# A recurrence with a per-channel decay, then a Fourier mix: one running sum less in batches 2 and 3, its exponentials moved one partition down by a DMA

## The chip, the core and the metric

The kernel runs on one core of one Trainium2 chip. The core has five engines with their own instruction streams: TensorE (PE in the profile; its weight loads are PEld), VectorE (DVE), ScalarE (ACT), GpSimd (POOL) and SyncE (SP), which here only issues DMAs. Sixteen DMA engines move data between HBM and the on-chip memory SBUF, which has 128 partitions; TensorE writes to PSUM, of eight banks. The metric is the device time in microseconds; a run's time is that of the whole execution, and the profile's span reaches from its first instruction to its last.

## What is computed

Two steps, one behind the other, on 4 batches, 8 heads, 768 steps and 48 channels a head (8 x 48 = 384).

```python
for t in range(S):
    cur = einsum('bhd,bhe->bhde', u * k[t], v[t])
    y[t] = einsum('bhd,bhde->bhe', r[t], state + cur)
    state = w[t][..., None] * state + einsum('bhd,bhe->bhde', k[t], v[t])
# y laid out as x: batch x 768 x 384
mixed = real(fft(fft(x, axis=1), axis=2))
un_ = x + mixed
un  = (un_ - mean) / sqrt(var + 1e-6)              # over the 384
out = un_ + maximum(un @ w_ch1, 0) @ w_ch2         # 384 -> 1536 -> 384
```

## The kernel before

**Tiling.** A batch is cut into six chunks of 128 steps, which lie on the 128 partitions. Chunks are counted through, n = 6b + c, so that batches 2 and 3 are n = 12 to 23. Batch 0 is worked in pairs of chunks by a function of its own (`attention2`); all others go through `attention`.

**A chunk in `attention`.** ScalarE takes the logarithm of w into a bf16 tile (L931). TensorE multiplies it by two triangles of ones, which gives two running sums over the steps: with MSK the sum over the steps before t (tile `tce`, L933), with NLE minus the sum up to and with t (tile `tci`, L937). A further small matmul puts the chunk's total into eight more columns of `tci` (L946). ScalarE takes the exponential of `tce` where it lies in PSUM (L939) and that of `tci` into the SBUF tile E2 (L952). r is multiplied by the first exponential (L971, VectorE, since that operand is in PSUM) and k by the second (L974, on GpSimd or VectorE). Both products are transposed, in batches 0 to 2 by TensorE (L987, L993), in batch 3 by a transposing DMA (L979). Then come their product A (L1003), its masked copy `ah` (L1008), the state (L1029, decayed at L1037), y (L1050 and L1053) and the sum into the row buffer X (L1059). Beside that, r times k times u is summed into `dc` and multiplied with v.

**Folding and mixing.** `fold` adds and subtracts mirrored columns of X. `mix` does the Fourier step with matmuls against cosine and sine tables (L1117, then L1140), adds X into a tile UF (L1142), takes its mean and variance (L1146, L1148), subtracts the mean (L1152), transposes (by TensorE in batches 0 and 1, by DMA at L1169 in 2 and 3), multiplies by W1 (L1187), applies the relu when it moves the result to SBUF (L1194 on ScalarE or L1192 on VectorE), multiplies by W2 (L1205), adds UF (L1209) and writes a row block out (L1213). There are two X and two UF buffers, by the parity of the batch.

**Inputs.** Each chunk's w, k, r, v is one load of 192 KB (L587) into one of seven slots; W1 and W2 are loaded by GpSimd's DMA queue (L745), W1 asked for once a load of batch 0 has landed and its turn on GpSimd has come.

**The order.** `op()` records every operation with the engines that it may run on, a cost, what it reads and what it writes. The table ORDER lists, for each engine, the numbers of the operations in the order in which that engine issues them; the number is the place in which the program recorded it. Nothing is ordered at run time: an engine stops at an operation until the semaphores of what it depends on have come, and everything behind it in its list waits too. The costs are used only to place PSUM tiles in banks and to sort the waits. SP's list has 120 DMAs.

Of the kernel before, what the change touches and what calls it, by code (L numbers as in the profile page):

```python
# [7 lines left out]
ALU = mybir.AluOpType  # L8
# [15 lines left out]

PAIRED = (0, 2, 4)
# [33 lines left out]
    "act": (  # L59
# [13 lines left out]
    "dve": (  # L73
# [15 lines left out]
    "pool": (  # L89
# [11 lines left out]
}  # L101


class _Tile:


    __slots__ = ("bank", "ops", "pool", "n_done", "end")

# [1173 lines left out]
```

## Time and profile before

| | |
|---|---|
| median of 3 runs | 186.04 us (184.61 to 190.06) |
| profiled execution, its time | 187.16 us |
| profiled execution, its span | 185.4 us |
| DMA engines, share of the span: queue of SP | 64.8% |
| DMA engines, share of the span: queue of GpSimd | 6.7% |
| mean granted TensorE clock | 0.989 |

The span is what the views divide; the time has the start and the end of the execution around it. A busy TensorE is not a TensorE at its peak, since the ends of matmuls are modelled and overlap, so the distance between the starts of neighbouring matmuls in an unbroken run is the better measure of what one costs. A share of the DMA engines is the time that packets took, summed over the sixteen and divided by sixteen times the stretch.

### The profile page before, as it was taken

How to read it: one execution, taken by the hardware profiler on the slowest of the kernel's cores; microseconds unless marked ns; L12 is line 12 of the kernel's file. 1: busy time of each engine (PE TensorE's matmuls, PEld its weight loads, DVE VectorE, ACT ScalarE, POOL GpSimd, SP SyncE). 2: the span in 40 equal slices, each digit the busy share in tenths (PEclk: the TensorE clock that was granted, in tenths of full speed). 3: DMA queues.
4: the chain of work that ended last, by engine and by line, in shares of the span. 5: the costliest groups of instructions: out<-in, count | busy, mean ns of one | idle time of the engine just before them, and what ended most of it. 6: DMA issues, size and time to landing. Idle time of an engine off the chain costs nothing.

```text
span 185.4 us, 4736 instructions
## 1 busy us (share of the span) xinstructions
PE 176.7 (95%) x1824; PEld 126.0 (68%) x1824; DVE 151.6 (82%) x360; ACT 128.7 (69%) x303; POOL 106.6 (58%) x128
## 2 busy tenths in 40 slices
PE   5999999997999999999999999999999999999993
PEld 2355676754788768767785777758788666887771
DVE  7979999999499999999999999999897297180043
ACT  5989999996799577899588789726745513627120
POOL 2359999799958826999694659868645000000000
PEclk9999999998799999999999999999999999999999
DMA  6999998999999899899498399692811005412033
GB/s 158 325 301 257 218 194 176 193 194 186 209 211 196 162 196 216 195 224 212 89 213 174 70 234 164 116 183 56 205 46 42 4 0 139 117 42 88 0 127 127
DMA packets 102600, 29.01 MB, mean 157 GB/s; under 512 B 98865, under 2 KB 102066, under 8 KB 102450
## 3 DMA queue, kind: packets, MB, share of 16 engines
q1 hardware_dynamic: 102034, 26.36, 64.8%
q0 software_dynamic: 544, 2.36, 6.7%
q8 instruction: 14, 0.23, 0.5%
q14 instruction: 8, 0.07, 0.1%
HBM read 23.59 MB, written 4.72 MB: 153 GB/s over the span
## 4 chain that ended last, share of the span: by engine, by line
PE 74%; DVE 9%; ACT 7%; DMA 6%; issue 2%; POOL 1%; POOLq 0%; DVEq 0%; ACTq 0%
PE bank L1205 24%; PE bank L1187 24%; DMA w<-in_moe_w_ch_dram 6%; PE bank L1140 5%; PE bank L1117 3%; DVE ah L856 2%; PE bank L1003 2%; PE bank L1226 2%; PE bank L1053 2%; PE bank L1248 2%; ACT rkt L550 1%; PE bank L1050 1%; ACT lb L541 1%; DVE xf L527 1%; PE bank L933 1%
## 5 line engine op out<-in xcount | busy, mean ns | idle before, releaser
L1187 PE MATMUL bank<-unt,w 128*128 128x384 bf16 x288 | 57.5, 335 | 1.0 <-DMA w<-in_moe_w_ch_dram 0.8
L1194 ACT ACTIVATE ht<-bank 128x384 bf16<-128x384 f32 x88 | 39.9, 496 | 24.4 <-PE bank L1187 24.0
L1205 PE MATMUL bank<-w,ht 128*128 128x384 bf16 (+2 forms) x300 | 53.0, 320 | 0.0
L1187 PEld LDWEIGHTS bank<-unt,w 128*128 128x128 bf16 x288 | 38.5, 145 | 8.3 <-DMA w<-in_moe_w_ch_dram 1.0
L1205 PEld LDWEIGHTS bank<-w,ht 128*128 128x128 bf16 x300 | 28.0, 98 | 15.6
L1209 DVE SCALAR_TENSOR_TENSOR osb<-bank,rstd,uf 128x384 f32<-128x384 f32 (+2 forms) x25 | 14.4, 594 | 17.8 <-PE bank L1205 13.3
L1008 DVE TENSOR_TENSOR ah<-bank,msk 128x512 bf16<-128x512 f32 x36 | 23.2, 678 | 0.9 <-PE bank L1003 0.7
L527 POOL TENSOR_TENSOR rkh<-in_k,e 128x384 bf16<-128x384 f32 x20 | 19.9, 997 | 5.6 <-ACT e L952 5.3
L527 POOL TENSOR_TENSOR rk<-rk,ub 128x384 f32<-128x384 f32 x18 | 18.6, 1038 | 5.5 <-DVE rk L527 2.4
L527 POOL TENSOR_TENSOR vtd<-in_v,dc 128x384 f32<-128x384 f32 (+1 forms) x22 | 18.1, 827 | 3.7 <-DVE dc L960 3.7
L527 POOL TENSOR_TENSOR rk<-in_r,in_k 128x384 f32<-128x384 f32 x18 | 18.2, 1020 | 0.0
L541 ACT ACTIVATE un<-uf,agg 128x384 bf16<-128x384 f32 x20 | 12.1, 615 | 7.1 <-DVE agg L1148 7.1
L550 ACT ACTIVATE rkt<-bank 128x512 bf16<-128x512 bf16 x24 | 15.1, 633 | 1.6 <-PE bank L987 1.6
L527 POOL TENSOR_TENSOR sd<-x 128x385 f32<-128x385 f32 x9 | 9.4, 1046 | 11.2 <-DVE sd L527 5.4
L1142 DVE TENSOR_TENSOR uf<-bank,x 128x384 f32<-128x384 f32 x24 | 12.9, 549 | 2.4 <-PE bank L1140 2.2
L527 POOL TENSOR_TENSOR xf<-sd 128x382 bf16<-128x382 f32 (+1 forms) x9 | 10.4, 1164 | 4.5 <-DVE sd L527 4.3
L1146 DVE BATCH_NORM_STATS2 bst<-uf 128x6 f32<-128x384 f32 x24 | 12.7, 546 | 0.1
L939 ACT ACTIVATE bank<-bank 128x384 f32<-128x384 f32 x18 | 8.8, 493 | 5.7 <-PE bank L933 5.7
L1059 DVE TENSOR_TENSOR x<-bank,vtd 128x384 f32<-128x384 f32 x18 | 9.7, 547 | 3.3 <-PE bank L1053 3.3
L541 ACT ACTIVATE lb<-in_w 128x384 bf16<-128x384 f32 (+1 forms) x21 | 12.1, 576 | 0.3 <-PE bank L798 0.2
L541 ACT ACTIVATE vb<-in_v 128x384 bf16<-128x384 f32 x22 | 11.4, 532 | 0.0
L952 ACT ACTIVATE e<-bank 128x392 f32<-128x392 f32 (+1 forms) x18 | 8.9, 497 | 2.5 <-DVE bank L1037 1.1
(167 smaller groups left out, 356.4 us busy)
## 6 DMA issues: line engine op xcount, KB each, us to landing
out_dram<-osb SPq DMA_DIRECT2D x23, 192.0 KB, 2.3
in_w<-in_w_dram SPq DMA_DIRECT2D x18, 192.0 KB, 4.3
in_k<-in_k_dram SPq DMA_DIRECT2D x18, 192.0 KB, 4.0
in_r<-in_r_dram SPq DMA_DIRECT2D x18, 192.0 KB, 3.9
in_v<-in_v_dram SPq DMA_DIRECT2D x18, 192.0 KB, 3.8
w<-in_moe_w_ch_dram POOLq DMA_DIRECT2D x2, 1152.0 KB, 10.6
in_w<-in_w_dram SPq DMA_DIRECT2D x3, 384.0 KB, 4.6
in_k<-in_k_dram SPq DMA_DIRECT2D x3, 384.0 KB, 4.6
```

Source lines behind the costliest of these rows:

```text
L527: return lambda e: e.tensor_tensor(out=o, in0=a, in1=b, op=f)
L541: return lambda e: e.activation(o, a, f, **kw)
L550: {"act": lambda e: e.activation(o(), i(), ACTF.Copy), "dve": lambda e: e.tensor_copy(out=o(), in_=i())}, **kw)
L1008: masked[n] = op("dve", v_1(512), lambda e, x=x: e.tensor_tensor(out=ah[:, x:H:2, :], in0=ps(ta[x])[:, :].rearrange("p (h t) -> p h t", t= ...
L1059: op("dve", v_1(DM), lambda e: e.tensor_tensor(out=xb[:, c, 0:DM], in0=ps(ty)[:, 0:DM], in1=vtd[:, :, :].rearrange("t h d -> t (h d)"), op ...
L1140: return e.matmul(ps(t)[:, 0:DM], (hcs if kb < NP else HCR)[:, j, a:a + 128], DTM[:, j, :], start=(j == 0), stop=(j == 2))
L1142: op("dve", v_1(DM), lambda e, kb=kb, t=t: e.tensor_tensor(out=uf[:, kb, :], in0=ps(t)[:, 0:DM], in1=xb[:, kb, 0:DM], op=ALU.add), r=[t, ( ...
L1146: op("dve", v_1(DM), lambda e, kb=kb, bs=bs: e.bn_stats(bs[:, :], uf[:, kb, :]), r=[("UF", i, kb)], w=[("BST", n % 4)])
L1187: ins = e.matmul(ps(t)[:, 0:384], W1[:, m, j:HID:NJ], unt[:, :, m, :], start=(m == 0), stop=(m == NM - 1))
L1194: "act": lambda e, j=j, t=t, ht=ht: e.activation(ht[:, j, :], ps(t)[:, 0:384], ACTF.Relu, scale=-1.0)},
L1205: ins = e.matmul(ps(t)[:, 0:hi - lo], ht[:, j, 128 * x:128 * x + 128], W2[:, j, lo:hi], start=(j == 0), stop=(j == NJ - 1))
L1209: op("dve", v_1(hi - lo) + 64, lambda e, kb=kb, t=t, o=o, lo=lo, hi=hi: e.scalar_tensor_tensor(out=o[:, lo:hi], in0=ps(t)[:, 0:hi - lo], s ...
```

## The change

For n of 12 and more (SHIFT_N), the first running sum is not computed. ScalarE takes a second exponential of the other sum, with the opposite sign, and writes it in float32 over the chunk's w in its input slot. Since the sum up to and with step t - 1 is the sum over the steps before t, a DMA on SP's queue copies partitions 0 to 126 of it to partitions 1 to 127 of a new tile E1; row 0 of E1 was set to 1 at the start and is not written again. r is multiplied by E1, which is in SBUF, so that the product may run on GpSimd as well as on VectorE. A second part, which takes the chunk's total decay out of the same exponentials by eight small DMAs, is written but switched off (DECAY_N is 99), so the small total matmul stays.

In all batches, the normed residual (UF in the kernel before) is written over the row buffer X, of which there are now three, by b modulo 3, and the two tiles of UF go. The scratch of the trigonometric tables moves from UF[1] to X[2]. Some costs of the planner are changed, the Pool and the DVE may both take one product of `attention2` as before but at another cost, and the whole ORDER table is new: in it eight of the twelve products with r are on GpSimd and four on VectorE. SP's list has 132 entries. W1 and W2 keep their conditions.

```diff
+SHIFT_N, DECAY_N = 12, 99
...
+    NS = 3
...
-    X = [sb("x%d" % i, [NC, DM + 4], FP32) for i in range(2)]
+    X = [sb("x%d" % i, [NC, DM + 4], FP32) for i in range(3)]
...
-    UF = [sb("uf%d" % i, [NC, DM], FP32) for i in range(2)]
+    E1 = [sb("e1_%d" % i, [H, D], FP32) for i in range(NS)]
+    WE = [sb("we%d" % i, [H], FP32) for i in range(NS)]
...
+        for i in range(NS):
+            op(None, {"pool": 390, "dve": 160}, fill(E1[i][0:1, :, :], 1.0), w=[("E1", i)])
+            op(None, {"pool": 90, "dve": 50}, fill(WE[i][:, :], 0.0), w=[("WE", i, h) for h in range(H)])
...
-        tce, tci = g.tile("a"), g.tile("a")
-        o = op("pe", mm(DM), lambda e: e.matmul(ps(tce)[:, 0:DM], MSK[:, :], L[:, :, 0:D]),
-               r=["MSK", ("LB", i2)], w=[tce])
...
+        turned, moved = n >= SHIFT_N, n >= DECAY_N and not last
+        ne = DM if last or moved else DM + H
+        ew, eq = INB["w"][i3], n % NS
+        if turned:
+            tci = g.tile("a")
...
+        o = op("pe", mm(DM), lambda e: e.matmul(ps(tci)[:, 0:DM], NLE[:, :], L[:, :, 0:D]),
+               r=["NLE", ("LB", i2)], w=[tci])
+        if turned:
+            if n - 2 in masked:
+                o.deps.add(masked[n - 2])
+            op("act", a_ps(DM) + 20, lambda e: e.activation(ew.rearrange("p h d -> p (h d)"), ps(tci)[:, 0:DM], ACTF.Exp, scale=-1.0),
+               r=[tci], w=[("in", "w", i3)])
+            op("sp", 620, lambda e: e.dma_start(E1[eq][1:128, :, :], ew[0:127, :, :]), r=[("in", "w", i3)], w=[("E1", eq)],
+               sem="e1%d" % eq, xfer=520)
...
+        if turned:
+            vec(DM, tt(rh[:, :, 0:D], E1[eq][:, :, :], rt[:, :, :], ALU.mult), r=[("in", "r", i3), ("E1", eq)], w=[("RH", i4)])
...
             op("dve", v_1(DM), lambda e, kb=kb, t=t: e.tensor_tensor(
-                out=uf[:, kb, :], in0=ps(t)[:, 0:DM], in1=xb[:, kb, 0:DM], op=ALU.add),
-               r=[t, ("X", i, kb)], w=[("UF", i, kb)])
+                out=uf[:, kb, 0:DM], in0=ps(t)[:, 0:DM], in1=uf[:, kb, 0:DM], op=ALU.add),
+               r=[t], w=[("X", ix, kb)])
```

The part of SP's new order that the prediction counts is this, from the first shift (s) to the last, with l a load, o an output, t the transposing DMA of a chunk and u that of a normed half batch:

```
s l l l l s l l l l l o l s o l l s l l l l l o l l l o s o l l l s
l l l l l l l l s l l l s t l t l l l o s l l s o o l t t u o l u s s
```

More of the change, by code (lines that the diff above doesn't have):

```diff
@@ L277, in _land @@
         for a, b in sw:
+            b -= 1500
             if t + dur <= a:
@@ L492, in bass_rwkv6_finch__then__fnet_fourier_mix_kernel @@
     CP = sb("cp", [1], FP32)
-    sc_u = UF[1].rearrange("p a b -> p (a b)")
+    sc_u = X[2].rearrange("p a b -> p (a b)")
     sc_h = HT[1].rearrange("p a b -> p (a b)").bitcast(FP32)
@@ L647, in fills @@
             for lo, hi, n, z in ((0, 64, "XFn", "XFz"), (446, 512, "XFo", "XFz2")):
-                op(None, {"pool": 250, "dve": 180}, fill(XF[i][:, :, lo:hi], 0.0),
+                op(None, {"pool": 370, "dve": 180}, fill(XF[i][:, :, lo:hi], 0.0),
                    w=[(z, i)] + [(n, i, c) for c in range(NC)])
-            op(None, {"pool": 100, "dve": 60}, fill(X[i][:, :, DM:DM + 4], 0.0), w=[("X", i, c) for c in range(NC)])
+        for i in range(3):
+            op(None, {"pool": 100, "dve": 60}, fill(X[i][:, :, DM:DM + 4], 0.0), w=[("X", i, c) for c in range(NC)]
+               + ([("TF", q) for q in range(NP)] if i == 2 else []))
+        for i in range(NS):
+            op(None, {"pool": 390, "dve": 160}, fill(E1[i][0:1, :, :], 1.0), w=[("E1", i)])
+            op(None, {"pool": 90, "dve": 50}, fill(WE[i][:, :], 0.0), w=[("WE", i, h) for h in range(H)])
     MAGIC = 12582912.0
@@ L742, in weights @@
     def weights():
-        for n, T, x, d, f in (("W1", W1, moe_w_ch1.rearrange("(q p) n -> p q n", p=128), 940, 7100),
-                              ("W2", W2, moe_w_ch2.rearrange("(p q) n -> p q n", p=128), 940, 7700)):
+        for n, T, x, d, f in (("W1", W1, moe_w_ch1.rearrange("(q p) n -> p q n", p=128), 940, 8400),
+                              ("W2", W2, moe_w_ch2.rearrange("(p q) n -> p q n", p=128), 940, 8400)):
             asked[n] = op("pool", d, lambda e, T=T, x=x: e.dma_start(T[:, :, :], x), w=[n], sem=n, xfer=f)
@@ L805, in attention2 @@
             rk, dc = RK[s[x]], DC[s[x]]
-            vec(DM, tt(rk[:, :, :], rt[:, x], kt[:, x], ALU.mult), r=rin + kin, w=[("RK", s[x])])
+            op(None, {"pool": p_1(DM) + 200, "dve": v_1(DM)}, tt(rk[:, :, :], rt[:, x], kt[:, x], ALU.mult), port=("dve",),
+               r=rin + kin, w=[("RK", s[x])])
             vec(DM, tt(rk[:, :, :], rk[:, :, :], UB[:, :, :], ALU.mult), r=[("RK", s[x]), "UB"], w=[("RK", s[x])])
@@ L928, in attention @@
         s_in, s_out = ST[(c + 1) % 2], ST[c % 2]
-        xb = X[b % 2]
+        xb = X[b % 3]
         pre = [("EXPS", n)] if n < LOG_FIRST else []
         op("act", a_sb(DM), act(L[:, :, 0:D], wt[:, :, :], ACTF.Ln), r=[("in", "w", i3), "LOGEXP"], w=[("LB", i2)])
-        tce, tci = g.tile("a"), g.tile("a")
-        o = op("pe", mm(DM), lambda e: e.matmul(ps(tce)[:, 0:DM], MSK[:, :], L[:, :, 0:D]),
-               r=["MSK", ("LB", i2)], w=[tce])
-        if n - 2 in masked:
-            o.deps.add(masked[n - 2])
-        op("pe", mm(DM), lambda e: e.matmul(ps(tci)[:, 0:DM], NLE[:, :], L[:, :, 0:D]),
-           r=["NLE", ("LB", i2)], w=[tci])
-        op("act", a_ps(DM) + 20, lambda e: e.activation(ps(tce)[:, 0:DM], ps(tce)[:, 0:DM], ACTF.Exp), w=[tce] + pre)
-        if not last:
+        turned, moved = n >= SHIFT_N, n >= DECAY_N and not last
[3 more added lines that the diff above has]
+            tci = g.tile("a")
+        else:
+            tce, tci = g.tile("a"), g.tile("a")
+            o = op("pe", mm(DM), lambda e: e.matmul(ps(tce)[:, 0:DM], MSK[:, :], L[:, :, 0:D]),
+                   r=["MSK", ("LB", i2)], w=[tce])
+            if n - 2 in masked:
[3 more added lines that the diff above has]
+        if turned:
+            if n - 2 in masked:
+                o.deps.add(masked[n - 2])
+            op("act", a_ps(DM) + 20, lambda e: e.activation(ew.rearrange("p h d -> p (h d)"), ps(tci)[:, 0:DM], ACTF.Exp, scale=-1.0),
+               r=[tci], w=[("in", "w", i3)])
+            op("sp", 620, lambda e: e.dma_start(E1[eq][1:128, :, :], ew[0:127, :, :]), r=[("in", "w", i3)], w=[("E1", eq)],
+               sem="e1%d" % eq, xfer=520)
+            if moved:
+                for h in range(H):
+                    lo = 64 * (h % 2)
+                    op("sp", 70, lambda e, h=h, lo=lo: e.dma_start(WE[eq][lo:lo + D, h:h + 1], ew[127:128, h, :]),
+                       r=[("in", "w", i3)], w=[("WE", eq, h)], sem="we%d" % eq, xfer=60)
+        else:
+            op("act", a_ps(DM) + 20, lambda e: e.activation(ps(tce)[:, 0:DM], ps(tce)[:, 0:DM], ACTF.Exp), w=[tce] + pre)
+        if not last and not moved:
             def tot(e):
@@ L950, in attention @@
             op("pe", mm(1, 5), tot, r=["ONE", "IDB", "PB0", "PB", ("LB", i2)], w=[tci])
-        ne = DM if last else DM + H
         op("act", a_ps(ne), lambda e: e.activation(E2[i2][:, 0:ne], ps(tci)[:, 0:ne], ACTF.Exp), r=[tci],
            w=[("E2", i2)] + pre)
+        if moved:
+            we = WE[eq]
         rk, rku, dc, vtd = RK[i2], RK[i2], DC[i2], VTD[n % 4]
@@ L969, in attention @@
            r=[("in", "v", i3)], w=[("VB", n % 4)])
-        op("dve", v_1(DM), lambda e: e.tensor_tensor(
-            out=rh[:, :, 0:D], in0=ps(tce)[:, 0:DM].rearrange("t (h d) -> t h d", d=D), in1=rt[:, :, :], op=ALU.mult),
-           r=[("in", "r", i3), tce], w=[("RH", i4)])
+        if turned:
+            vec(DM, tt(rh[:, :, 0:D], E1[eq][:, :, :], rt[:, :, :], ALU.mult), r=[("in", "r", i3), ("E1", eq)], w=[("RH", i4)])
+        else:
+            op("dve", v_1(DM), lambda e: e.tensor_tensor(
+                out=rh[:, :, 0:D], in0=ps(tce)[:, 0:DM].rearrange("t (h d) -> t h d", d=D), in1=rt[:, :, :], op=ALU.mult),
+               r=[("in", "r", i3), tce], w=[("RH", i4)])
         vec(DM, tt(kh[:, :, 0:D], kt[:, :, :], e2[:, :, :], ALU.mult),
@@ L1005, in amat @@
             return ins
-        op("pe", 207, amat, r=[("KTB", i4), ("RTB", i4)], w=ta, tiled=True)
+        op("pe", 232, amat, r=[("KTB", i4), ("RTB", i4)], w=ta, tiled=True)
         for x in range(2):
@@ L1039, in decay @@
                                        in1=we[:, :].unsqueeze(2).to_broadcast([128, H, D]), op=ALU.mult)
+            wer = [("WE", eq, h) for h in range(H)] if moved else [("E2", i2)]
             s_flat = s_out[:, :, :].rearrange("p q x -> p (q x)")
             if stay and c < NC - 2:
-                op("dve", v_1(DM), lambda e: decay(e, ps(tds)[:, 0:DM]), r=[("E2", i2)], w=[tds])
+                op("dve", v_1(DM), lambda e: decay(e, ps(tds)[:, 0:DM]), r=wer, w=[tds])
                 evict(lambda: s_flat, lambda: ps(tds)[:, 0:DM], DM, r=[tds], w=[("ST", c % 2)])
             else:
-                op("dve", v_1(DM), lambda e: decay(e, s_flat), r=[tds, ("E2", i2)], w=[("ST", c % 2)])
+                op("dve", v_1(DM), lambda e: decay(e, s_flat), r=[tds] + wer, w=[("ST", c % 2)])
         def ymat(e):
@@ L1061, in attention @@
             in1=vtd[:, :, :].rearrange("t h d -> t (h d)"), op=ALU.add),
-           r=[ty, ("VTD", n % 4)], w=[("X", b % 2, c)])
+           r=[ty, ("VTD", n % 4)], w=[("X", b % 3, c)])
         fold(b, c)
@@ L1067, in fold @@
         i = b % 2
-        xf, xb = XF[i], X[i]
+        ix = b % 3
+        xf, xb = XF[i], X[ix]
         if b < FOLD:
             vec(192, tt(xf[:, c, 64:256], xb[:, c, 0:192], xb[:, c, 384:192:-1], ALU.add),
-                r=[("X", i, c)], w=[("XFe", i, c)])
+                r=[("X", ix, c)], w=[("XFe", i, c)])
             vec(191, tt(xf[:, c, 256:447], xb[:, c, 1:192], xb[:, c, 383:192:-1], ALU.subtract),
-                r=[("X", i, c)], w=[("XFo", i, c)])
+                r=[("X", ix, c)], w=[("XFo", i, c)])
             if c == NC - 1:
                 op("act", 96, lambda e: e.activation(xf[:, :, 63], xb[:, :, 192], ACTF.Copy),
-                   r=[("X", i, x) for x in range(NC)], w=[("XFn", i, x) for x in range(NC)])
+                   r=[("X", ix, x) for x in range(NC)], w=[("XFn", i, x) for x in range(NC)])
             return
@@ L1082, in fold @@
         sd = SD[:, z, :, :]
-        both = [("X", i, p), ("X", i, c)]
+        both = [("X", ix, p), ("X", ix, c)]
         vec(DM, tt(sd[:, 0, 0:DM + 1], xb[:, p, 0:DM + 1], xb[:, c, 0:DM + 1], ALU.add), r=both, w=[("SD", z, 0)] + HALVES)
@@ L1095, in mix @@
         i = b % 2
-        xf, hcs, xb, uf = XF[i], HCS, X[i], UF[i]
+        ix = b % 3
+        xf, hcs, uf = XF[i], HCS, X[ix]
         for jn, j in enumerate((0, 2, 1)):
@@ L1152, in mix @@
             op(None, {"act": a_sb(DM) + 95, "dve": v_2(DM) + 60},
-               {"act": act(un, uf[:, kb, :], ACTF.Identity, scale=-1.0, bias=agg[:, kb, 0:1]),
-                "dve": ts(un, uf[:, kb, :], agg[:, kb, 0:1], -1.0, ALU.subtract, ALU.mult)}, port=("dve",),
-               r=[("UF", i, kb), ("AGG", i, kb)], w=[("UN", iu, kb % 3)])
+               {"act": act(un, uf[:, kb, 0:DM], ACTF.Identity, scale=-1.0, bias=agg[:, kb, 0:1]),
+                "dve": ts(un, uf[:, kb, 0:DM], agg[:, kb, 0:1], -1.0, ALU.subtract, ALU.mult)}, port=("dve",),
+               r=[("X", ix, kb), ("AGG", i, kb)], w=[("UN", iu, kb % 3)])
             hf = kb // 3
```

16 lines of the change are left out of this document (8 added, 8 removed), and 122 rows, old and new, of the table ORDER.

## The prediction

> **What bounds the kernel now.** I read the page's top first, then the sums by stretches of 20 us, then the chain that ended last, then the DMA part.
>
> ```profile
> span 185.4 us, 4736 instructions
> PE 176.7 (95%) x1824; PEld 126.0 (68%) x1824; DVE 151.6 (82%) x360; ACT 128.7 (69%) x303; POOL 106.6 (58%) x128
> ```
>
> ```profile
> core 0: us, PE busy (x) PEld busy (x) DVE busy (x) ACT busy (x) POOL busy (x), PEclk, DMA share, GB/s
> 40.00:60.00 20.00, 18.45 (x199) 13.70 (x197) 16.77 (x41) 17.27 (x42) 17.14 (x20) 0.91 1.03 202
> 60.00:80.00 20.00, 19.75 (x224) 14.66 (x223) 19.68 (x40) 14.88 (x40) 13.42 (x15) 1.00 0.93 192
> 80.00:100.00 20.00, 19.56 (x215) 14.38 (x212) 19.85 (x42) 16.31 (x39) 16.65 (x18) 1.00 0.84 178
> 100.00:120.00 20.00, 20.00 (x210) 14.69 (x211) 18.95 (x43) 16.61 (x44) 15.71 (x16) 1.00 0.82 150
> 120.00:140.00 20.00, 20.00 (x196) 14.99 (x195) 19.01 (x42) 11.05 (x27) 12.06 (x13) 1.00 0.57 127
> ```
>
> Two things are short at once. TensorE works nearly without a gap from 60 us on. The sixteen DMA engines, in the second last column, are full until 60 us and 82 to 93% full until 120 us, which is the stretch in which batches 2 and 3 load and in which the change adds twelve transfers.
>
> ```profile
> 33.83 10.87 DMA w<-in_moe_w_ch_dram
> 44.74 3.05 PE bank L1187 x9
> ...
> 143.16 1.09 PE bank L1117 x13
> ...
> 152.30 5.20 PE bank L1205 x32
> ...
> 181.72 0.61 DVE osb L1209
> ```
>
> The chain (start, duration, what) says when: W1 lands at 44.7, and from there to 181.7 the end is TensorE's work one after the other, with 3.7 us of last additions and output behind it. A 384-column matmul in an unbroken run takes 5.20/32 = 0.1625 us, a 193-column one 1.09/13 = 0.084. The first nine after W1 took 3.05 where nine make 1.46: the granted clock was 0.91 over that stretch, and coming back from a pause cost 1.6 us.
>
> **Part by part: TensorE, ScalarE, VectorE, GpSimd.**
>
> ```profile
> L971 DVE TENSOR_TENSOR rkh<-bank,in_r 128x384 bf16<-128x384 f32 x18 | 9.6, 545 | 0.1
> L527 POOL TENSOR_TENSOR rkh<-in_k,e 128x384 bf16<-128x384 f32 x20 | 19.9, 997 | 5.6 <-ACT e L952 5.3 <-ACT e L784 0.3
> L939 ACT ACTIVATE bank<-bank 128x384 f32<-128x384 f32 x18 | 8.8, 493 | 5.7 <-PE bank L933 5.7
> L1003 PE MATMUL bank<-rkt 48*128 48x128 bf16 x144 | 6.1, 218 | 0.0
> L933 PE MATMUL bank<-lb,msk 128*128 128x384 bf16 x18 | 5.6, 327 | 0.0
> ```
>
> For the twelve chunks of batches 2 and 3 the L933 sum goes: 12 x 0.1625 = 1.95 us of TensorE, all on the path that sets the end. The exponential of L939 stays, from the other running sum, written to SBUF: 12 x 0.49 as now, nothing gained. The product with r (L971) gets both operands from SBUF; by the new order eight of twelve are on GpSimd at about the 0.997 of the like product with k, so 8 us of GpSimd against 8 x 0.545 = 4.4 us of VectorE, which takes twelve more hidden-layer evictions in exchange. Neither engine is full in the table, so I cost these at nothing by themselves; if that cover went, it would be the 8 us. The new order also has about 2.1 us more of TensorE's work (one sum of each kind, a transposed r, one A, one state product, three y's; an estimate from 0.1625 a sum, 0.7 an A, and the count of matmuls in the others) ahead of the first W1 product, where TensorE waits anyway: the 40 to 60 row shows 1.55 us idle, so that is what it can win. Keeping the normed rows in the row buffer makes batch 3's rows wait for batch 0's outputs; in the new VectorE order those stand well ahead of batch 3's first row, and with three buffers batch 2 waits for nothing. That, and seven small fills, I cost at nothing. The decay part is switched off (99 is past the last chunk, 23).
>
> **The shift itself.** It moves 127 rows of 1,536 bytes from partitions 0..126 to 1..127. No transfer in the trace has 127 rows, so its price must be bounded.
>
> ```profile
> DMA packets 102600, 29.01 MB, mean 157 GB/s; under 512 B 98865, under 2 KB 102066, under 8 KB 102450
> ...
> out_dram<-osb SPq DMA_DIRECT2D x23, 192.0 KB, 2.3
> ...
> in_w<-in_w_dram SPq DMA_DIRECT2D x18, 192.0 KB, 4.3
> ...
> out_dram<-osb SPq DMA_DIRECT2D x1, 128.0 KB, 1.7
> rkt<-rkh SPq DMA_TRANSPOSE x6, 3.4
> ...
> out_dram<-osb SPq DMA_DIRECT2D x1, 64.0 KB, 1.5
> osb<-in_u_dram SPq DMA_DIRECT2D x1, 1.5 KB
> ```
>
> Between 512 bytes and 2 KB there are 102066 - 98865 = 3201 packets. The 25 outputs have 128 rows each; 25 x 128 = 3200, and the one left is the row of u. So these transfers go as one packet a row, and u's, the only transfer here whose rows don't divide by sixteen, was one packet and sat on one engine. Next, a stretch from 164 to 167 us with nothing in it but one output:
>
> ```profile
> DMA packets 144, 0.20 MB, mean 66 GB/s; under 512 B 16, under 2 KB 144, under 8 KB 144
> q1 hardware_dynamic: 144, 0.20, 17.7%
> out_dram<-osb SPq DMA_DIRECT2D x1, 192.0 KB, 2.0
> ```
>
> That is 128 packets of a row and 16 small ones, one for each engine, and 17.7% x 3 us x 16 = 8.5 us of engine time: 0.53 us when sixteen share it, 8.5 us when one has it all, and 2.0 - 0.53 = 1.5 us of latency. So a shift moves data for between 0.53 us (like the output) and 8.5 us (like u, on one engine). 127 cannot be cut into sixteen equal parts, or into any; the transfer that it resembles in this is u, and I take 8.5 us on one engine. The Trainium skill says the same of a transfer issued by SP, in "DMA: Bandwidth & Descriptors", section "Why a DMA increments its semaphore by 16 and not by 1": the engines used are the largest number up to sixteen that divides the count of the slowest dimension, so that 127 partitions go to one. The trace agrees as far as it reaches, with u's single packet; by the rule the sum is the long one below, and by an even spread the short one.
>
> What queues behind: every input load spreads over all sixteen engines, so each load, transpose or output issued after a shift has a part that stands behind it on that engine. SP issues in order and stops at each shift until its exponential is done; behind it stand loads of r, k, v, w. GpSimd (or VectorE) stops at the product with r until the shift has landed, with the products for the next chunks behind it, and TensorE stops at the transposed r or at A.
>
> **The sum with one engine.**
>
> ```profile
> 63.58 0.47 ACT L939 ACTIVATE bank<-bank 128x384 f32<-128x384 f32 x1 [1.02 <-PE bank L933]
> ```
>
> This is the exponential of batch 2's first chunk: the first shift starts at about 63. Then I count, in the new SP order, what the loaded engine must move. A load costs it, by the row of 60 to 80 us, 196.6 KB at 192/0.93 = 206 GB/s, or 0.95 us; an output 0.53. From the first shift to the eighth (batch 3's second chunk) stand 8 shifts, 34 loads and 5 outputs: 68 + 32.3 + 2.7 = 103, so the eighth lands at 166. Those waits that I can follow up to there (the sum of the next chunk stands on TensorE behind the transposed r of the last) take some 4 us and lie beside the 5 to 8 loads queued between, so they are free.
>
> From there it is a loop. The transposing DMA of batch 3's first chunk stands behind the eighth shift: 3.4; then thirteen matmuls of 0.084 and a sum, 1.3; exponential 0.5; latency 1.5; shift 8.5; two loads 1.9; the tenth shift 8.5. That is 26: 192. The next sum stands in TensorE's order behind chunk 3's A: product on GpSimd 1.0, transpose 3.4, A (6.1/144 x 16 = 0.7) and eight or so matmuls 1.5, exponential 0.5, latency 1.5, the last two shifts 17, product on VectorE 0.5, transpose 3.4: 29.5, so the last A starts at 221.
>
> Behind the last A the order still has 26 W1 groups of 3, 38 W2 groups (140 matmuls, the narrow ones of the last tile counted by width), 18 of 384 and 24 of 193 columns: (78 + 140 + 18) x 0.1625 + 24 x 0.084 + some 0.6 = 41. TensorE has idled before it, so the slow restart of 1.6 comes again. With the 3.7 at the end: 63 + 103 + 26 + 29.5 + 41 + 1.6 + 3.7 = 267.8. The profiled execution took 187.16 with a span of 185.4, so 1.8 lies around the span, and it is 1.1 over the median of the runs, 186.04: about **269 us**.
>
> **The rivals.** (1) The shift spreads like an output. For it: every large transfer of the trace does. Against it: u's packet and the odd 127. Then twelve times 0.53 = 6.4 us a DMA engine fits into the 7 to 18% that are free from 60 to 120 us, and the time is 187.16 - 1.95 - 1.55 - 1.1, about 183: faster, but within 2%. (2) The same, and the work put ahead of W1 also keeps the clock up: 1.6 us less, 181, faster by more than 2%. For it the 0.91; against it, W1 is asked for behind one product more on GpSimd. It decides if TensorE has no pause before W1 lands. (3) Spread, but each shift holds SP until its exponential is there: above about 0.7 us a shift, twelve use up the 8 us or so of free DMA time in 60 to 120, and at 1.2 us they cost some 6: 189 to 190. (4) One engine, with waits that lie less beside each other or more: one more loop of 8 us per batch makes 285 and four 300; if batch 2's six shifts stayed hidden behind TensorE's backlog, 6 x 8.5 of the sum and the loads with them shrink by 35 or so: 234. This is the range of the forecast, not another case.
>
> **How the numbers follow.** One engine 0.85; rival (1) 0.06; (2) 0.04; (3) 0.05, four fifths of it over 2%. 2% is about what a measurement of this kernel can tell from no change. So faster 0.04, same 0.07, slower 0.89. The likeliest case gives 269 and runs from 234 to 300; leaving out rivals (1) to (3) leaves out 0.15, and some 0.04 more lies beyond the two ends.
>
> **What would show it.** Right: packets of the shifts over 100 us of time in the page's DMA part but a low mean share after 63 us, 8 to 10 us from issue to landing for `e1<-in_w`, GpSimd and VectorE waiting for DMA before the product with r, loads of batch 3 landing in well over 4.3 us, a granted clock below the 1.00 of the rows above, and a dense last 45 us. Wrong: a landing of 2 to 3 us for the shift; then look at where W1 lands and at idle TensorE before it. If the landing is long but the time is short of 230, the in-order waits were weaker than I have them.

## The result, and the profile after

| | before | after |
|---|---|---|
| median | 186.25 us of 4 runs (184.61 to 190.06) | 275.06 us of 4 runs (274.73 to 276.16) |
| ratio | | 1.482, 95% interval 1.471 to 1.493 |
| profiled execution, its time and span | 187.16 and 185.4 us | 274.75 and 272.9 us |
| mean granted TensorE clock | 0.989 | 0.869 |

The change costs 89 us. The forecast was 269 us in a range of 234 to 300. First the head of the page of the changed kernel: the span, the busy times, TensorE's granted clock in 40 slices, and the DMA part.

```profile
span 272.9 us, 4727 instructions
PE 198.6 (73%) x1812; PEld 135.7 (50%) x1812; DVE 159.4 (58%) x369; ACT 127.5 (47%) x297; POOL 108.2 (40%) x132
PEclk9999999999868888686769866886888668999999
DMA packets 104135, 31.34 MB, mean 115 GB/s; under 512 B 98877, under 2 KB 103602, under 8 KB 103986
q1 hardware_dynamic: 103570, 28.70, 50.0%
```

No engine has much more to do than before (VectorE 159.4 us against 151.6, GpSimd 108.2 against 106.6; TensorE's 198.6 against 176.7 are twelve matmuls fewer at a lower clock), and none is near its limit any more: TensorE has gone from 95% to 73% of the span. The shifts are the 103602 - 98877 = 4725 packets between 512 bytes and 2 KB less the 3201 of before: 1524, twelve times 127, a packet a row. Together the DMA engines are half idle. The sums by stretches of 20 us of the same run have TensorE in the second column, and the clock and the DMA share third and second from the end:

```profile
60.00:80.00 20.00, 13.57 (x116) 9.30 (x115) 11.13 (x23) 8.57 (x24) 6.44 (x6) 0.83 0.40 85
80.00:100.00 20.00, 10.70 (x89) 6.98 (x87) 9.11 (x20) 10.49 (x24) 7.51 (x9) 0.91 0.46 106
...
200.00:220.00 20.00, 10.82 (x84) 7.94 (x81) 6.02 (x12) 7.86 (x19) 1.03 (x2) 0.83 0.30 37
220.00:240.00 20.00, 18.61 (x144) 12.71 (x145) 14.08 (x29) 4.94 (x13) 11.75 (x13) 0.83 0.19 50
240.00:260.00 20.00, 20.00 (x125) 14.93 (x124) 11.92 (x29) 7.06 (x18) 0.15 (x1) 1.00 0.30 89
```

Before, the stretch from 60 to 80 us had 19.75 us of TensorE and 93% of the DMA engines; now it has 13.57 and 40%, and so on until 220 us. A DMA share of 0.40 looks like room. It isn't, as a closer look shows. This is the DMA part of a window from 128 to 135 us that lies nearly inside one shift; its two rows of 40 slices (0.175 us each) are the busy tenths of the sixteen engines and what they moved:

```profile
DMA  0100003899993000000000000267999500000000
GB/s 18 26 0 26 26 26 74 168 181 252 266 205 77 24 26 26 26 26 26 26 26 18 26 26 26 64 136 171 250 263 206 117 31 26 26 18 26 26 18 26
in_w<-in_w_dram SPq DMA_DIRECT2D x2, 192.0 KB, 7.8
in_r<-in_r_dram SPq DMA_DIRECT2D x1, 192.0 KB, 10.5
```

Most slices read 0 tenths and 26 or 18 GB/s: three or two rows of 1,536 bytes in 0.175 us, one behind the other on one engine. Two bursts of over 250 GB/s are loads' shares on the other engines, done in about 1 us each, and then those engines stand. The loads themselves land only after 7.8 and 10.5 us, because each has a sixteenth behind the shift.

The chain that ended last (start, duration, what) names the shift (`e<-in_w`), and SP's issues of loads (L592) between two shifts:

```profile
64.09 2.63 SPq L592
66.78 3.66 SPq L592
70.48 3.26 SPq L592
74.46 10.75 DMA e<-in_w
...
95.01 14.04 DMA e<-in_w
...
212.00 9.14 DMA rkt<-rkh
```

From 63 us to 221 about three quarters of this chain are transfers and SP's issues of transfers, and TensorE's work one after the other, which made the end before from 44.7 us on, makes it only after. An issue of a load takes SP 2.6 to 3.7 us here; in these rows SP does not wait for an operand, it stands inside its own issues. The two groups of products with r wait, in all, for (us, times, longest):

```profile
POOL rkh L532 <- DMA e<-in_w: 73.6, 8, 16.6
DVE rkh L532 <- DMA e<-in_w: 28.3, 4, 8.2
```

In the kernel before, the product with r waited 0.1 us in all eighteen chunks.

### The profile page after: what moved, and what is told of

Its sections match the earlier page's. It is cut to its first block, busy times and chain, and to the rows that moved or that the text cites. A ratio compares the mean times of both kernels' runs of the same rounds, so it can differ in the third digit from the quotient of the medians.

```text
span 272.9 us, 4727 instructions
## 1 busy us (share of the span) xinstructions
PE 198.6 (73%) x1812; PEld 135.7 (50%) x1812; DVE 159.4 (58%) x369; ACT 127.5 (47%) x297; POOL 108.2 (40%) x132
## 2 busy tenths in 40 slices
DMA packets 104135, 31.34 MB, mean 115 GB/s; under 512 B 98877, under 2 KB 103602, under 8 KB 103986
## 4 chain that ended last, share of the span: by engine, by line
PE 31%; DMA 28%; SPq 23%; DVE 9%; ACT 4%; issue 2%; POOL 1%; DVEq 0%; POOLq 0%
DMA e<-in_w 17%; SPq L592 17%; PE bank L1224 12%; PE bank L1242 10%; DMA rkt<-rkh 7%; SPq L1250 2%; DMA in_v<-in_v_dram 2%; DMA in_r<-in_r_dram 2%; DVE ah L1042 2%; SPq L961 2%; SPq L584 2%; PE bank L1154 2%; PE bank L1037 2%; PE bank L1177 1%; DVE xf L532 1%
## 5 line engine op out<-in xcount | busy, mean ns | idle before, releaser
L1242 PE MATMUL bank<-w,ht 128*128 128x384 bf16 (+2 forms) x300 | 62.9, 359 | 0.0
L1231 ACT ACTIVATE ht<-bank 128x384 bf16<-128x384 f32 x76 | 35.0, 491 | 31.7 <-PE bank L1224 31.7
L532 POOL TENSOR_TENSOR rkh<-e,in_r 128x384 bf16<-128x384 f32 x8 | 7.9, 992 | 73.6 <-DMA e<-in_w 73.6
L1021 PE MATMUL bank<-idw,rkh 128*128 128x128 bf16 x48 | 5.3, 240 | 29.1 <-POOL rkh L532 22.4
L1246 DVE SCALAR_TENSOR_TENSOR osb<-bank,rstd,x 128x384 f32<-128x384 f32 (+2 forms) x25 | 14.6, 594 | 16.6 <-PE bank L1242 11.4
L1021 PEld LDWEIGHTS bank<-idw,rkh 128*128 128x128 bf16 x48 | 3.4, 105 | 30.9 <-issue 20.2
L1037 PE MATMUL bank<-rkt 48*128 48x128 bf16 x144 | 8.8, 261 | 13.3 <-DMA rkt<-rkh 7.9
L532 POOL TENSOR_TENSOR rkh<-in_k,e 128x384 bf16<-128x384 f32 x16 | 16.0, 1002 | 4.7 <-ACT e L981 3.4
L532 POOL TENSOR_TENSOR xf<-sd 128x384 bf16<-128x384 f32 (+1 forms) x9 | 9.8, 1096 | 13.9 <-DVE sd L532 13.6
L546 ACT ACTIVATE un<-x,agg 128x384 bf16<-128x384 f32 x20 | 11.5, 616 | 7.8 <-DVE agg L1185 7.6
```

Source lines behind the costliest of these rows:

```text
L532: return lambda e: e.tensor_tensor(out=o, in0=a, in1=b, op=f)
L546: return lambda e: e.activation(o, a, f, **kw)
L1021: ins = e.transpose(psb(trr)[:, 128 * h:128 * h + 128], rflat[:, 128 * h:128 * h + 128], IDB[:, :])
L1037: ins = e.matmul(ps(ta[x])[:, 128 * q:128 * q + 128], kT[64 * x:64 * x + D, q, :], rT[64 * x:64 * x + D, q, :])
L1231: "act": lambda e, j=j, t=t, ht=ht: e.activation(ht[:, j, :], ps(t)[:, 0:384], ACTF.Relu, scale=-1.0)},
L1242: ins = e.matmul(ps(t)[:, 0:hi - lo], ht[:, j, 128 * x:128 * x + 128], W2[:, j, lo:hi], start=(j == 0), stop=(j == NJ - 1))
```

## The experiments

Two theories stood at the start. **One engine**: 127 rows cannot be cut into equal parts, so a shift lies on one DMA engine, and that engine is too full for the loads. **The hop**: the detour through SBUF as such, or the new order of the work, costs the time. Behind the first stands a second question: does the loaded engine cost time because products wait for the shift, because loads stand behind it, or whatever is done about both?

Each experiment is a single run, beside the kernel before at 185.1 to 186.4 us; only the split shift and the kernel without shifts have six runs each. Since runs of the kernel before lie between 184.6 and 190.1 us, a few microseconds between two single runs prove nothing by themselves.

**Ten transfers by themselves.** No part of the kernel but a source tile, ten transfers from partition 0 on to partition 1 on (the first, of 128 rows, in place), each issued when VectorE has been released by the one before.

```diff
+ROWS = (128, 127, 126, 125, 124, 122, 120, 112, 64, 63)
...
+                eng.dma_start(b[s:s + n, i, :], a[0:n, :]).then_inc(d[i], 16)
```

> Ten transfers by themselves, each of n rows of 1,536 bytes from partitions 0..n-1 to 1..n (128: without the step down), one after the other, each waited for. Nothing of the reference is computed; ones are written out. One engine takes all 127 rows (theory): with 1.5 us of latency and 0.068 us a row on the fullest engine, landing after about 2.0 us for 128 rows (16 engines, 8 each), 10.2 for 127 (one engine), 2.1 for 126 (14), 3.2 for 125 (5 x 25), 3.6 for 124 (4 x 31), 5.7 for 122 (2 x 61), 2.0 for 120 and 112, 1.8 for 64, 2.0 for 63 (9 x 7). Rival, that moving rows one partition down is slow whatever the count: 10 us for all but 128. Rival, that the transfer spreads and is slow only among the loads of the kernel: 2 us for all.

VectorE's timeline; the number in brackets is its wait for the transfer, issue and release included:

```profile
3.57 0.06 DVE L21 MEMSET z<- 128x1 f32 x1 [2.31 <-DMA b<-a]
13.92 0.06 DVE L21 MEMSET z<- 128x1 f32 x1 [10.29 <-DMA b<-a]
16.90 0.06 DVE L21 MEMSET z<- 128x1 f32 x1 [2.92 <-DMA b<-a]
20.83 0.06 DVE L21 MEMSET z<- 128x1 f32 x1 [3.88 <-DMA b<-a]
25.36 0.06 DVE L21 MEMSET z<- 128x1 f32 x1 [4.46 <-DMA b<-a]
31.73 0.06 DVE L21 MEMSET z<- 128x1 f32 x1 [6.32 <-DMA b<-a]
```

128, 127, 126, 125, 124 and 122 rows: 127 takes 10.29 us, 126 takes 2.92 with the same step of one partition. The order of the others is that of the largest divisor up to sixteen: 14, 5, 4 and 2 for 126, 125, 124 and 122, so 9, 25, 31 and 61 rows an engine. The 120, 112, 64 and 63 rows, not shown, took 2.86, 2.53, 2.17 and 2.56 us. All but the 127 took 0.3 to 0.9 us longer than expected; their order, and the 10.29, are as expected. The Trainium skill, in "DMA: Bandwidth & Descriptors", section "Why a DMA increments its semaphore by 16 and not by 1", gives this rule, and these six agree with it.

**One row less in the kernel.** 126 rows; row 127 of E1 stays at the 1 of the start, for which the fill at the start now covers all of E1.

```diff
-            op("sp", 620, lambda e: e.dma_start(E1[eq][1:128, :, :], ew[0:127, :, :]), r=[("in", "w", i3)], w=[("E1", eq)],
+            op("sp", 620, lambda e: e.dma_start(E1[eq][1:127, :, :], ew[0:126, :, :]), r=[("in", "w", i3)], w=[("E1", eq)],
```

> The changed kernel with one row less in each shift, 126 in place of 127; the last row of E1 keeps a one, so r's last row of each of the twelve chunks is scaled wrongly. One engine per shift (theory): 126 rows go to 14 engines with 9 each, 0.6 us, and the time falls from 275 to about 184. Rival, that the added hop and the engines that wait for it in order are what costs: one row changes nothing, 275. Rival, that the step of one partition is slow: 275.

190.25 us. One row fewer of 127 takes 85 of the 89 us away. The expected 184 was missed: something else seems to cost some 4 us, and the kernel is still not faster than before.

**122 rows, and half a row.** The same edit with 122 rows, which two engines share, and with 127 rows of four heads (768 bytes).

> The same with 122 rows, 2 x 61; five rows of E1 keep ones, so five rows of r are scaled wrongly in each chunk. Theory: two engines with 61 rows each, 4.2 us a shift in place of 8.6, so about half of the loss comes back: 275 - 12 x 4.4 = 222, some 10 less where the waits now hide: 212 to 228. Rivals as before: 275; if any count but 127 spreads over sixteen: 184.

> The changed kernel with 127 rows, but half of each, 768 bytes (heads 0 to 3; the other half of E1 keeps ones, so r of heads 4 to 7 is not scaled). Theory: still one engine, but a row takes about 0.037 us in place of 0.068 (between the 0.027 and 0.046 of 512 and 1,024 bytes), 4.7 us a shift: 215 to 230. If it were a fixed cost of each row, 275; if the hop alone, 275.

226.64 and 229.72 us. Halving what the busiest engine has to move, by a second engine or by half the bytes, gives back about half: 48 and 45 of 89 us. So it is neither a fixed price for a row nor for an issue. Both times lie in the ranges that the theory gave.

**Two transfers, and none.** First the 127 rows as 112 and 15, one behind the other from SP, on one semaphore. Then no shift: TensorE computes both sums and ScalarE both exponentials, E1 in SBUF, with the rest of the change as it is.

```diff
+            o = op("sp", 620, lambda e: [e.dma_start(E1[eq][1:113, :, :], ew[0:112, :, :]),
+                                         e.dma_start(E1[eq][113:128, :, :], ew[112:127, :, :])],
...
+            o.nd_ = 2
```

```diff
+            def both(e):
+                e.matmul(ps(tce)[:, 0:DM], MSK[:, :], L[:, :, 0:D])
+                return e.matmul(ps(tci)[:, 0:DM], NLE[:, :], L[:, :, 0:D])
...
-            op("act", a_ps(DM) + 20, lambda e: e.activation(ew.rearrange("p h d -> p (h d)"), ps(tci)[:, 0:DM], ACTF.Exp, scale=-1.0),
-               r=[tci], w=[("in", "w", i3)])
-            op("sp", 620, lambda e: e.dma_start(E1[eq][1:128, :, :], ew[0:127, :, :]), r=[("in", "w", i3)], w=[("E1", eq)],
+            oa = op("act", a_ps(DM) + 20, lambda e: e.activation(E1[eq].rearrange("p h d -> p (h d)"), ps(tce)[:, 0:DM], ACTF.Exp),
+                    r=[tce], w=[("E1", eq)])
+            op("sp", 20, lambda e: e.nop())
```

> The changed kernel with each shift of 127 rows issued as two transfers, of 112 rows and of 15 rows, one behind the other from SP; nothing else differs. By the theory (a count of 127 rows leaves one DMA engine, so 8.5 us of data per shift) both parts spread over 16 and 15 engines; alone, 112 rows took 2.5 us from issue to release, so the pair should take about 3 to 3.5 us, and the time should come near the 190.25 us of the 126-row shift, a little above for the second issue on SP (0.8 us each, 12 of them, not all on the path): 190 us, 187 to 194. If the hop through memory as such cost the time, or the new order, it stays at 275 us; if the order of the work carries a good part of it, over 210 us. Under 186 us it would beat the kernel before.

> The changed kernel's order, its normed rows in the residual's place and its products from rows in SBUF are kept, but in batches 2 and 3 TensorE computes both running sums again and ScalarE writes both exponentials; no shift is issued. The output is the reference's. It tells how the 4 us by which the 126-row shift (190.25) stands above the kernel before (186.2) are made up. If they come from the hop (12 shifts of 2.9 us and the waits behind them), 184 to 187 us; if the new order costs them, 188 to 191 us. If the order carried a good part of the 89 us, it would be far above 200 us.

The split shift takes 193.9 us (192.91 to 194.43), at the upper end of what was expected, 1.042 of before with an interval of 1.038 to 1.047; without shifts it takes 191.84 (191.24 to 194.32), 1.031 (1.025 to 1.036). The two parts of a split shift land in 2.7 and 2.6 us (last column) in the run's DMA part, where the whole one has no landing at all, and GpSimd's products wait 10.6 us for them in place of 73.6:

```profile
e<-in_w SPq DMA_DIRECT2D x12, 168.0 KB, 2.7
e<-in_w SPq DMA_DIRECT2D x12, 22.5 KB, 2.6
```

```profile
POOL rkh L534 <- DMA e<-in_w: 10.6, 6, 3.5
```

This divides the 89 us (medians): 191.8 - 186.4 = 5.5 for what the change does without a shift (that run still computes the first sum), 193.9 - 191.8 = 2.1 for twelve shifts that spread, and 275.1 - 193.9 = 81 for the one engine. The 2.1 may belong to the second issue of each shift: 126 rows in one transfer took 190.25, in its single run. Expected for the run without shifts were 184 to 187, or 188 to 191 if the order costs; its 191.84 lies just above the second. The sums of the first two stretches, before any shift, first of the kernel before, then of the run without shifts:

```profile
0.00:20.00 20.00, 17.19 (x159) 8.94 (x159) 17.78 (x73) 16.63 (x31) 10.86 (x23) 1.00 1.00 256
20.00:40.00 20.00, 19.45 (x358) 14.37 (x358) 19.85 (x43) 19.53 (x46) 18.41 (x24) 1.00 0.99 194
```

```profile
0.00:20.00 20.00, 15.14 (x148) 8.02 (x149) 17.80 (x73) 16.00 (x31) 9.18 (x21) 1.00 0.89 226
20.00:40.00 20.00, 18.30 (x343) 12.87 (x343) 19.08 (x36) 16.25 (x37) 15.60 (x20) 1.00 0.91 184
```

By 40 us TensorE has been busy 3.2 us less, ScalarE 3.9 and GpSimd 4.5, with the clock at 1.00: the new order starts more thinly. The loss shows at W1. GpSimd asks for it at 36.94 us (33.83 before), so it lands at 47.7 in place of 44.7, and the chain has TensorE's first product with W1 at 50.1, where before it stood at 44.74. Between 47.7 and 50.0 TensorE still does the work that the new order has put ahead of it:

```profile
36.94 0.98 POOL L755 DMA_DIRECT2D w<-in_moe_w_ch_dram  x1
```

```profile
50.09 2.07 PE bank L1231 x12
```

From there on both runs take about the same, 141 us to the end of the span, so these 5.3 us are nearly all of the 5.5. Why GpSimd comes to W1 later stays open.

**Nobody waits for it.** As the run without shifts, but 127 rows of other data (the tile of u, not the exponentials that the expectation names) are sent at the shift's place in SP's list to the shifted rows of the free input slot, and no product reads them.

```diff
-            op("sp", 20, lambda e: e.nop())
+            o = op("sp", 620, lambda e: e.dma_start(ew[1:128, :, :], UB[0:127, :, :]), r=["UB"], w=[("in", "w", i3)],
+                   sem="nb%d" % n, xfer=520)
+            o.deps.add(oa)
```

> As the run without shifts, but a transfer of 127 rows from the exponentials to the shifted place is issued at the point in SP's list where the shift stood, and no product waits for it; only the reload of that slot, and the end, come behind it. The exponential that the product reads is written by ScalarE. It separates two ways in which the slow shift costs time. If most of the 89 us comes from the products that wait for the shift, about 190 us (185 to 200). If it comes from the one loaded engine, on which the loads issued behind each shift have to wait their turn for 8.5 us, 240 to 275 us. I hold both to act and the wait to be the larger: 200 us.

269.76 us, where I had held 200 for likeliest. That nobody waits for the shift saves next to nothing; the waits move to the loads, and to the transposes behind them:

```profile
ACT lb L546 <- DMA in_w<-in_w_dram: 28.0, 5, 11.4
...
ACT vb L546 <- DMA in_v<-in_v_dram: 23.0, 5, 11.1
PEld bank L1046 <- DMA rkt<-rkh: 19.7, 4, 11.1
```

**Another queue; tiles of its own; half of the shifts.** In the first, ScalarE issues the changed kernel's own shift right behind its exponential. In the second, the transfer that nobody waits for goes to three tiles that nothing else uses, so that no reload of a slot waits for it. In the third, only batch 3 shifts, and batch 2 does as the run without shifts.

```diff
-            op("sp", 620, lambda e: e.dma_start(E1[eq][1:128, :, :], ew[0:127, :, :]), r=[("in", "w", i3)], w=[("E1", eq)],
+            op("act", 620, lambda e: e.dma_start(E1[eq][1:128, :, :], ew[0:127, :, :]), r=[("in", "w", i3)], w=[("E1", eq)],
```

```diff
+    NBT = [sb("nbt%d" % i, [H, D], FP32) for i in range(NS)]
...
+            o = op("sp", 620, lambda e: e.dma_start(NBT[eq][1:128, :, :], UB[0:127, :, :]), r=["UB"], w=[("NBT", eq)],
```

> The changed kernel, but each shift of 127 rows is issued by ScalarE, right behind its second exponential, and so goes through ScalarE's DMA queue instead of SP's. In the changed kernel SP's own issues took 139.8 us of the 157 us from 63 to 220 us (73 of them; 57.4 us for 73 in the kernel before): SP stood still inside its issues of loads. Two theories. Order in one queue: rows of loads stand behind the shift's rows in SP's queue and SP stops when that queue is full; with a queue of their own the shifts delay only the product that waits for them, about 200 us (190 to 215). Capacity of the one engine: 12 shifts of 8.5 us are 102 us, and the same engine has to carry its sixteenth of all loads and outputs, so it has no room whatever queue they come by; 255 us or more (245 to 275). I hold the capacity for likelier, since the time without shifts (191.8) plus 6 to 7 us a shift gives 270.

> As the run in which a transfer of 127 rows is issued and no product waits for it (269.76 us), but it goes into tiles of its own (three, in turn), so that no reload of an input slot waits for it either. What the products read is written by ScalarE. If the one engine and the queue behind it carry the time, it stays at 260 to 272 us. If SP's wait for the reload of the slot carried it, 192 to 205 us.

> The changed kernel with the shift of 127 rows in batch 3 alone (6 of the 12); for batch 2 TensorE computes both sums and ScalarE both exponentials. The output is the reference's. If each shift costs its own time on the one engine, less the time in which that engine had room, the time lies half way between the run without shifts (191.8) and the changed kernel (275.1): 233 us, 222 to 242. If a single stop (the first shift, or the last) sets the end, it is near one of the two.

272.12, 273.81 and 234.83 us. The reload was not it; 273.81 is even 1.8 us above the range named for the one engine. Half the shifts cost half: 43 of the 83 us between no shift and all twelve, so about 7 us each. And a queue of their own does not help the shifts, which have one now (q10). A window from 76 to 85 us of that run lies inside its second shift:

```profile
q10 hardware_dynamic: 124, 0.19, 5.6%
in_k<-in_k_dram SPq DMA_DIRECT2D x1, 192.0 KB, 16.1
```

124 rows of the shift took 5.6% of sixteen engines for 9 us, or 8.1 us: of one engine nearly all of the window. A load of k, which comes by SP's queue and has nothing to do with the shift's, took 16.1 us to land.

**Both at once: another queue, and nobody waits.** The transfer into tiles of its own, issued by ScalarE.

> The transfer of 127 rows is issued by ScalarE, so by another queue than the loads', into tiles of its own; no product waits for it, and what the products read is written by ScalarE. Its one wait is that every third transfer into a tile waits for the first. It takes both roads away on which the slow shift has cost time so far: loads behind it in SP's queue (noreload, 273.8 us, where nobody waits for it) and products waiting for it (272.1 us with a queue of its own). If the two roads are all there is, 195 to 215 us. If the engine itself has no room, it stays at 250 us or more: in the run without shifts a packet of 192 bytes took 15.6 ns, so the engine's sixteenth of a load (64 packets) takes 1.0 us, the 43 loads between 63 and 220 us of the changed kernel 43 us, and beside the 101 us of shifts the engine would be full there for about 150 of 157 us. I hold the second for likelier.

264.39 us. With both roads closed the kernel is 11 us quicker than the changed one, not 60 or more; where those 11 come from stays open. The loads land late in this run too, and so do the transposes (3.4 us before):

```profile
in_r<-in_r_dram SPq DMA_DIRECT2D x18, 192.0 KB, 7.3
rkt<-rkh SPq DMA_TRANSPOSE x6, 11.1
```

So the engine's room is what is short. In the DMA part of the changed kernel, cut to 63 to 220 us, stand

```profile
in_v<-in_v_dram SPq DMA_DIRECT2D x12, 192.0 KB, 6.0
e<-in_w SPq DMA_DIRECT2D x12, 190.5 KB
in_k<-in_k_dram SPq DMA_DIRECT2D x11, 192.0 KB, 5.3
in_r<-in_r_dram SPq DMA_DIRECT2D x11, 192.0 KB, 3.8
out_dram<-osb SPq DMA_DIRECT2D x11, 192.0 KB, 3.4
in_w<-in_w_dram SPq DMA_DIRECT2D x9, 192.0 KB, 8.2
```

By the prediction's prices that is 12 x 8.5 + 43 x 0.95 + 11 x 0.53 = 149 us of work for one engine in 157 us, with the transposes still to come. Moving the wait, or the queue, takes nothing off that sum. It takes all twelve shifts to lie on the same engine. The last two bear that out: both are issued by 204.1 us, and their products with r start at 211.29 and 219.53, so the second shift is carried behind the first and lands 8.2 us after it.

```profile
211.29 0.56 DVE L532 TENSOR_TENSOR rkh<-e,in_r 128x384 bf16<-128x384 f32 x1 [8.19 <-DMA e<-in_w]
```

**GpSimd's queue.** The changed kernel's shift, whole, issued by GpSimd a product or two ahead of its use.

```diff
-            op("sp", 620, lambda e: e.dma_start(E1[eq][1:128, :, :], ew[0:127, :, :]), r=[("in", "w", i3)], w=[("E1", eq)],
+            op("pool", 620, lambda e: e.dma_start(E1[eq][1:128, :, :], ew[0:127, :, :]), r=[("in", "w", i3)], w=[("E1", eq)],
```

> The changed kernel, but each shift of 127 rows, whole and in one transfer, is issued by GpSimd, a product or two ahead of where its result is used, and so goes by GpSimd's DMA queue, the one that W1 and W2 take. With ScalarE's queue in SP's place nothing was won (272.1 us). If a transfer of 127 rows sits on one engine whoever issues it, 260 to 285 us: the same load on the engine, and GpSimd held at its place besides. If GpSimd's queue cuts it over several engines, the time falls to the split shift's (193.9) and some more for what an issue costs GpSimd (not shown by any run so far for such a transfer; bounded below by nothing and above by some 2 us each, of which half is hidden, GpSimd being busy 57% of the split run): 194 to 206 us. The Trainium skill, in DMA: Bandwidth & Descriptors, section Why a DMA increments its semaphore by 16 and not by 1, says that some direct copies by GpSimd's queue use all sixteen engines with the count rounded up, and names 127 among them; by that rule the second case comes. I give it 0.6.

198.19 us. The same 127 rows, in one transfer, no longer load one engine: they land in 3.6 us, which one engine's 8.5 us of data do not allow.

```profile
e<-in_w POOLq DMA_DIRECT2D x12, 190.5 KB, 3.6
```

That a transfer of 127 rows by GpSimd's queue spreads is the exception that the same section of the Trainium skill's "DMA: Bandwidth & Descriptors" states; this run agrees. It is the other remedy beside the split, 4 us behind it in a single run. No version here beats the kernel before.

## Why the prediction was right

**The price of a shift.** Bounded between 0.53 us and 8.5, taken as 8.5 on one engine by its likeness to u's row. That likeness proved little, since a single packet lies on one engine whatever the rule for many rows is; the choice was right all the same. Shown: 10.29 us by itself, which less the 2.31 of 128 rows (0.53 of them data) leaves about 8.5 of data; and one row less, or a cut at 112, takes the cost away.

**The counting of one engine's work.** The sum took what the loaded engine must move in SP's order, and held the waits along the way free. This was the bold step, and the last runs show that it was the right one: who waits, and in which queue (SP's or ScalarE's), changes the time by 1 to 11 us of 89 while the engine is full. Its stations can be read off the products with r, which start when their shift has landed, in the timelines of VectorE and GpSimd:

```profile
164.72 0.56 DVE L532 TENSOR_TENSOR rkh<-e,in_r 128x384 bf16<-128x384 f32 x1 [7.10 <-DMA e<-in_w]
...
219.53 0.56 DVE L532 TENSOR_TENSOR rkh<-e,in_r 128x384 bf16<-128x384 f32 x1 [5.68 <-DMA e<-in_w]
```

```profile
191.57 0.99 POOL L532 TENSOR_TENSOR rkh<-e,in_r 128x384 bf16<-128x384 f32 x1 [6.07 <-DMA e<-in_w]
```

| station | forecast | measured |
|---|---|---|
| first shift | 63 | 63.3 (issue) |
| eighth landed | 166 | 164.7 |
| tenth landed | 192 | 191.6 |
| last product with r | 217.6 | 219.5 |
| last transpose landed | 221 | 225.4 |
| last A starts | 221 | 228.6 |
| from there to the end of the span | 46.3 | 44.3 |

**The last loop, and the end.** The term that was sized too small is the last loop, 29.5 us from the landing of the tenth shift to the last A: it took 37.0. The two last shifts in it cost about what was said. What was left out stands behind them. The last transpose comes in SP's list behind three outputs, is issued at 220.9, and takes 4.5 us to land, not 3.4. And the last A stands in TensorE's order behind the work of the chunk before, whose own A had to wait for its transpose until 221.4; from that A to the last one TensorE works 7.2 us without a wait:

```profile
221.39 0.61 PE L1037 MATMUL bank<-rkt 48*128 48x128 bf16 x8 [4.00 <-DMA rkt<-rkh]
...
228.56 0.40 PE L1037 MATMUL bank<-rkt 48*128 48x128 bf16 x8
```

What follows the last A, 41 + 1.6 + 3.7 = 46.3, was sized 2.0 us too large: it took 44.3, although the clock in the stretch from 220 to 240 us was 0.83. The two errors offset each other in part, so that the span of 267.8 came within 5.1 us of the measured 272.9.

**The signs named.** A low share after 63 us, the waits of GpSimd and VectorE, a clock below 1.00 and a dense last stretch came as said, and loads of w landed in 8.2 us from 63 us on. The packets of the shifts can be told from the rest only in the run on ScalarE's queue, where q10 took 2.4% of sixteen engines for 270.3 us, or 104 us; over 100 were forecast. The landing of the shift itself, forecast as 8 to 10 us, is not in the page; three of the chain's pieces are 10.6 to 10.8 us, near the 10.29 of a shift alone, and the one of 14.0 also stood behind an earlier shift.

**Where it would have been wrong.** The forecast's rival (1), a shift that spreads, stood at 183 us, within 2% of before. The split shift is that case, and took 193.9. Two of its steps failed. The new order was to win 3.5 us on TensorE and cost nothing by itself ("I cost these at nothing"), where the change without any shift lost 5.5, since W1's first product came 5.3 us later. And the shift's 6.4 us of DMA time were to fit into free slices, where twelve short shifts cost 2.1. Rival (3), at 189 to 190 us, is nearer in number, but not by its mechanism: it put the loss on SP held by shifts, and most of it is there without a shift.

## What to carry to other kernels

Before moving a tile by a partition, look at the number of rows: 127 on SP's or ScalarE's queue is one engine's work, while 112 + 15, or the same transfer from GpSimd, spreads. Price a DMA by the busiest engine, not by bytes over sixteen: a mean share of 40 to 50% hid an engine that had 149 us of work in 157. While that engine was full, neither moving the wait nor ScalarE's queue helped much; counting what it had to move from the first shift to the eighth gave 103 us, and it took 101.

## What had not been expected of the hardware

A queue of its own for the shifts gave a load no way past them. With the shifts on ScalarE's queue, the engine gave 8.1 of 9 us to a shift, and the load that took 16.1 us had been issued on SP's queue at 69.97, after the two shifts of 64.18 and 68.36. With one queue for both, the load that SP issued at 204.16 after the last two shifts took as long, 15.9. Both times count from the start of the issue, in which SP stood 6.5 and 7.7 us.

```profile
in_v<-in_v_dram SPq DMA_DIRECT2D x1, 192.0 KB, 15.9
```

SP is held by its issues. In the stretch from 63 to 220 us of the changed kernel its 73 issues took 139.8 us, added up issue by issue (a row of the timeline that joins several also holds the pauses between them). Two late ones are these:

```profile
204.16 7.73 SPq L592 DMA_DIRECT2D in_v<-in_v_dram  x1
212.00 7.29 SPq L1013 DMA_TRANSPOSE rkt<-rkh  x1
```

In the kernel before, the 73 issues from 63 us to its end took 57.4 us. Here an issue that took several us was the sign of an engine that was full, where the shares seemed to show room.
